# Rounding casts of converted weights moved to GpSimd, and five early copies to ScalarE, in a fused attention and expert kernel on one core

## The chip, the cores and the metric

The kernel runs on one core of a Trainium2 chip. The time is that of one execution on the device, in microseconds (us); the median of several runs is compared. A core has five engines, each with an instruction stream of its own, executed in order: TensorE (PE in the profile, its weight loads PEld), VectorE (DVE), ScalarE (ACT), GpSimd (POOL) and SyncE (SP, which here only issues DMAs). They meet by semaphores.

## The reference

Three stages, in fp32, on 4 batches of 576 positions, 2304 tokens in all:

```python
# attention: 8 heads of 64, window of 64 positions
scores = (q @ k.T) / sqrt(64); masked unless 0 <= i - j < 64
attn = exp(scores - max) / (sum + 1e-9);  x = attn @ v        # (2304, 512)
# dense layer: w_in (512, 2048), w_out (2048, 512)
h = x @ w_in;  g = h * tanh(softplus(h));  x = g @ w_out
# experts: 8, each w1 (512, 1024), w2 (1024, 512); one expert per token
e = argmax(x @ w_gate + modality_bias[modality])
out = gate[e] * (relu(x @ w1[e]) @ w2[e])
```

## The kernel before, in words

Large products are made of two-part numbers: a value is split into a high part (rounded to fp32r) and a low part (the rest), and three matmuls make one product (`hidden`, L338 to L342, and `output`, L377 to L379). So each weight has to be split first: the high part is a rounding copy, the low part is the value minus the high part.

The weights of the dense layer come from the host as 64-bit floats. A piece of 128x512 numbers is converted in `convert_a` by three operations on VectorE (a shift L300, and two that join masked words, L304 and L308), then `convert_b` makes the high part (L326, the line that the change touches) and hands back the arguments of the low part, which `convert_end` issues later on VectorE (L1004). There are 32 pieces. `convert_start(n)` issues n of the three operations; `convert_end` issues the low parts that are open, then the high parts of the pieces that are ready. Nothing is reordered: the schedule is the order in which the Python code issues.

Attention works in 36 steps of 64 positions. Step number `na` handles several positions in turn: scores for `na` (L142 adds the mask, L144), for the one before it the row maximum (VectorE, L159), its negation (GpSimd, L160) and four exponentials with their sums (ScalarE, L184), for the one before that the scaling: GpSimd adds 1e-9 to the sums (L198), VectorE takes the reciprocal (L199), GpSimd scales four blocks (L201). For the third position back TensorE turns the weights (`flip`, L211), a copy takes them out of PSUM (`flipped`, L216), and TensorE multiplies with the values (`values`, L227). `pt_copy` (L1016) chooses the engine of that copy: ScalarE if `na` is in `PT_ACT`, else VectorE. Then `done` copies the result (ScalarE, L239 with its low part L252 on VectorE for the first eight positions, later L245).

The first 12 steps (`PRE`) run attention alone, in `att_alone`, with a few operations of conversion: until about 45 us. The next 28 steps are mixed: each has one step of the dense layer (24 hidden matmuls, and from the third step on 12 output matmuls of the step two before), the activation (ScalarE L415 to L418 and L426, VectorE L420, L427, L428), the split of g (high part ScalarE L434, low part VectorE L435), one step of attention in two halves, `att_a` and `att_b`, and one piece converted in each half (`CONV` is 3), until the pieces are used up at about 155 us. In a half, the order is:

```python
def att_a(convs, *between):          # att_b: flipped, largest (L159, L160),
    ... done                         #   convert_end, convert_start, exps, values
    convert_end(); convert_start(convs)
    ... scale (L198, L199, L201), rest, scores, flip
```

After that come the rest of the dense layer, the routing and the experts.

Of the kernel before, what the change touches and what calls it, by code (L numbers as in the profile page):

```python
# [39 lines left out]
PRE = 12  # L40
AHEAD = 1
MASK_PE = 26
PT_ACT = range(PRE, 27)
RAW_AT = -1, 1, 3
V_AT = 1
REST = range(NG)
# [222 lines left out]
class Rounds:  # L269
# [43 lines left out]
    def convert_b(self, key, f):  # L313
        nc = self.nc
        src, j, half = key
        if src == "in":
            if j not in self.w1:
                self.w1[j] = self.w1_pool.tile([P, 2, KD, G], F32R, name="w1")
            hs = slice(2 * half, 2 * half + 2)
            parts = [self.w1[j][:, x, hs].rearrange("p a b -> p (a b)") for x in range(2)]  # L320
        else:
            if j not in self.w2:
                self.w2[j] = self.w2_pool.tile([P, 2, 2, D], F32R, name="w2")
            parts = [self.w2[j][:, x, half] for x in range(2)]
        hi, lo = parts
        nc.scalar.copy(hi, f)  # L326
        return lo, f, hi.bitcast(F32), ALU.subtract


# [603 lines left out]
def tile_kernel(tc, a):  # L933
    nc = tc.nc
    with ExitStack() as ctx:
# [22 lines left out]
        with tc.manual_schedule():  # L958
# [57 lines left out]
            def pt_copy():  # L1016
                if na in PT_ACT:
                    return nc.scalar.copy
                return nc.vector.tensor_copy
# [346 lines left out]
```

## Time and profile before

| | before |
|---|---|
| median of 3 runs | 748.85 us (747.72 to 749.16) |
| profiled execution | 749.38 us, of which the instructions span 747.6 us |
| TensorE (PE) busy | 719.3 us, 96% |
| VectorE (DVE) busy | 563.6 us, 75% |
| ScalarE (ACT) busy | 490.1 us, 66% |
| GpSimd (POOL) busy | 158.7 us, 21% |

The share of busy time is an average over stages. Times in the trace are counted from the start of the span. Matmuls are pipelined: the listed duration of one overlaps the next. On VectorE, too, an operation is listed as begun a little before the one ahead of it ends.

### The profile page before, as it was taken

To read this page: it belongs to the slowest core of one execution; us is meant where nothing else is said; L and a number is where in the kernel's file an instruction comes from. 1 tells how busy PE (TensorE), PEld (TensorE's weight loads), DVE (VectorE), ACT (ScalarE), POOL (GpSimd) and SP (SyncE) were. 2 spreads that over 40 slices of the span, in tenths; PEclk is the share of its full clock that TensorE was granted. 3 is DMA by queue.
4 is the path that set the end of the run, shared out by engine and by line. 5 is a ranking of instruction groups with operands and counts; after the bars stand their busy time and mean duration, and the time that the engine had idled before them with its cause. 6 is when DMAs were issued, how large, how long until landed. Compare 5 with 4: busy or idle time off the path is not lost. (4 is left out here: it accounts for less than half of the span.)

```text
span 747.6 us, 14044 instructions
## 1 busy us (share of the span) xinstructions
PE 719.3 (96%) x5123; PEld 648.6 (87%) x5123; DVE 563.6 (75%) x1323; ACT 490.1 (66%) x1018; POOL 158.7 (21%) x301
## 2 busy tenths in 40 slices
PE   5679999999999999999999999999999999999996
PEld 4568988998988899999998899998899999999995
DVE  4879999966565479889898988999987565555660
ACT  4568888888787677767776777676323546545452
POOL 5763223232322010101101011021123112220111
PEclk9999999999999999999999999999999999999999
DMA  8977667733241310000101000352011711111520
GB/s 258 270 218 229 218 211 225 219 122 79 78 121 58 120 53 1 29 29 29 58 1 37 21 29 29 113 168 59 30 57 57 268 43 58 57 39 34 198 86 32
DMA packets 42912, 75.51 MB, mean 101 GB/s; under 512 B 3857, under 2 KB 20241, under 8 KB 42706
## 3 DMA queue, kind: packets, MB, share of 16 engines
q1 hardware_dynamic: 30818, 56.01, 23.8%
q0 software_dynamic: 4480, 14.46, 5.7%
q10 hardware_dynamic: 7536, 4.06, 1.9%
q8 instruction: 42, 0.69, 0.4%
q14 instruction: 36, 0.29, 0.1%
HBM read 82.36 MB, written 13.39 MB: 128 GB/s over the span
## 5 line engine op out<-in xcount | busy, mean ns | idle before, releaser
L338 PE MATMUL h<-xh,w 128*128 128x256 f32 x576 | 166.8, 290 | 0.7 <-DVE y L428 0.7
L341 PE MATMUL h<-xl,w 128*128 128x256 f32 x576 | 163.6, 284 | 0.0
L342 PE MATMUL h<-xh,w 128*128 128x256 f32 x576 | 163.6, 284 | 0.0
L377 PE MATMUL acc<-w,g 128*128 128x512 f32 x288 | 115.4, 401 | 0.0
L338 PEld LDWEIGHTS h<-xh,w 128*128 128x128 f32 x576 | 110.9, 192 | 5.0 <-DVE y L428 1.1
L378 PE MATMUL acc<-w,g 128*128 128x512 f32 x288 | 112.6, 391 | 0.0
L341 PEld LDWEIGHTS h<-xl,w 128*128 128x128 f32 x576 | 111.1, 193 | 1.5
L379 PE MATMUL acc<-w,g 128*128 128x512 f32 x288 | 112.2, 390 | 0.0
L342 PEld LDWEIGHTS h<-xh,w 128*128 128x128 f32 x576 | 111.0, 193 | 0.0
L550 DVE CUSTOM_DVE_ANT_0 junk<-row,wg 128x512 bf16<-128x512 f32 x144 | 99.2, 689 | 2.7
L442 ACT ACTIVATE g<-h 128x512 fp32r<-128x512 f32 x36 | 21.5, 598 | 93.6 <-PE h L342 83.7
L341 PE MATMUL h<-xl,ew 128*128 128x256 f32 x288 | 81.6, 283 | 0.7 <-DVE xl L908 0.7
L342 PE MATMUL h<-xh,ew 128*128 128x256 f32 x288 | 81.5, 283 | 0.0
L338 PE MATMUL h<-xh,ew 128*128 128x256 f32 x288 | 81.5, 283 | 0.0
L415 ACT ACTIVATE y<-h 128x512 f32<-128x512 f32 x72 | 43.1, 599 | 58.0 <-PE h L342 56.2
L201 POOL TENSOR_SCALAR p<-p,r 128x128 f32<-128x128 f32 x144 | 64.1, 462 | 57.9 <-DVE r L199 54.1
L420 DVE SCALAR_TENSOR_TENSOR pq<-y,r 128x512 f32<-128x512 f32 x72 | 49.6, 689 | 28.9 <-ACT r L418 28.9
L629 POOL DMA_INDIRECT xs_dram<-row,posi x18 | 19.4, 1079 | 228.2 <-DVE row L620 92.2
L426 ACT ACTIVATE pq<-pq,mid 128x512 f32<-128x512 f32 x72 | 52.2, 726 | 22.9 <-DVE pq L420 18.7
L379 PEld LDWEIGHTS acc<-w,g 128*128 128x128 f32 x288 | 54.1, 188 | 11.9 <-DVE g L435 0.2
L435 DVE TENSOR_TENSOR g<-y,g 128x512 fp32r<-128x512 f32 x72 | 49.5, 687 | 17.6 <-ACT g L434 17.6
L377 PEld LDWEIGHTS acc<-w,g 128*128 128x128 f32 x288 | 54.3, 188 | 9.0
(216 smaller groups left out, 1653.2 us busy)
## 6 DMA issues: line engine op xcount, KB each, us to landing
s<-e_w SPq DMA_DIRECT2D x32, 1024.0 KB
v<-v SPq DMA_DIRECT2D x36, 256.0 KB
raw<-w_in SPq DMA_DIRECT2D x16, 512.0 KB
raw<-w_out SPq DMA_DIRECT2D x16, 512.0 KB
kt<-kT SPq DMA_DIRECT2D x17, 384.0 KB
qd<-qT SPq DMA_DIRECT2D x36, 128.0 KB
x_dram<-xs ACTq DMA_DIRECT2D x14, 256.0 KB
xraw<-x_dram SPq DMA_DIRECT2D x14, 256.0 KB
```

What stands on the lines that cost most here:

```text
L201: nc.gpsimd.tensor_scalar(p[:, c, :], p[:, c, :], r[:, c : c + 1], 0.0, ALU.mult, ALU.add)
L338: nc.tensor.matmul(h[:, f], w[:, 0, k, fs], xh[:, k], start=(k == 0), stop=False)
L341: nc.tensor.matmul(h[:, f], w[:, 0, k, fs], xl[:, k], start=False, stop=False)
L342: nc.tensor.matmul(h[:, f], w[:, 1, k, fs], xh[:, k], start=False, stop=(k == KD - 1))
L377: nc.tensor.matmul(acc[c], gh[:, 0, f, cs], w[:, 0, f], start=st, stop=False)
L378: nc.tensor.matmul(acc[c], gh[:, 0, f, cs], w[:, 1, f], start=False, stop=False)
L379: nc.tensor.matmul(acc[c], gh[:, 1, f, cs], w[:, 0, f], start=False, stop=en)
L415: nc.scalar.activation(y, h, AF.Tanh, scale=0.5)
L420: nc.vector.scalar_tensor_tensor(p, y, 1.0, r, ALU.add, ALU.mult)
L426: nc.scalar.activation(p, p, AF.Square, bias=self.c["mid"][:, 0:1])
L435: lo_engine.tensor_tensor(flat(t[:, 1]), g, flat(t[:, 0]).bitcast(F32), ALU.subtract)
L550: nc.vector.tensor_tensor_reduce(out=junk, in0=rows[c][:, 0:D], in1=self.wg[:, e], scale=1.0, scalar=0.0, op0=ALU.mult, op1=ALU.add, accum ...
```

## The change

The high part of the 32 converted pieces is made on GpSimd instead of ScalarE, and in five of the nine opening steps that have such a copy (4, 6, 8, 10, 11 of 3 to 11) the turned attention weights are copied by ScalarE instead of VectorE. Nothing else is changed.

```diff
-PT_ACT = range(PRE, 27)
+PT_ACT = 4, 6, 8, 10, 11, *range(PRE, 27)
...
         hi, lo = parts
-        nc.scalar.copy(hi, f)
+        nc.gpsimd.tensor_copy(hi, f)
         return lo, f, hi.bitcast(F32), ALU.subtract
```

GpSimd, in the mixed steps (L160 the negated maximum, L326 the casts, L198 the sums, L201 the scaling; the first rows belong to one step, the next to the step behind it):

```order
 L160 TENSOR_SCALAR mx_818<-mx_818 128x4
+L326 CAST w1_783<-cv_729 128x512
+L326 CAST w2_883<-cv_788 128x512
 L198 TENSOR_SCALAR r_891<-sm_838 128x4
 L201 TENSOR_SCALAR p_837<-p_837,r_891 128x128 x4
 L160 TENSOR_SCALAR mx_932<-mx_932 128x4
+L326 CAST w2_883<-cv_826 128x512
+L326 CAST w1_997<-cv_888 128x512
 L198 TENSOR_SCALAR r_1005<-sm_952 128x4
```

Two casts now stand one behind the other between the negated maximum and the sums of every mixed step with conversions.

ScalarE, at the start of the mixed steps (L216 the copy of the turned weights, L415 on the activation, L245 and L248 the attention output and its DMA):

```order
 L245 COPY xs_693<-o_659 128x4x64
-L326 CAST w2_695<-cv_589 128x512
 L216 COPY pt_719<-t_714 128x512
-L326 CAST w2_695<-cv_640 128x512
 L415 ACTIVATE y_732<-h_668 128x512
```

The copies of the turned weights no longer stand between two casts.

ScalarE, in the opening (L184 the exponentials, L239 the high part of the attention output):

```order
 L239 CAST xh_275<-o_358 128x4x64
-L326 CAST w1_386<-cv_243 128x512
 L184 ACTIVATE p_392,sm_393<-s_acc_326,mx_372 128x128 x4
+L216 COPY pt_405<-t_acc_381 128x512
 L239 CAST xh_275<-o_408 128x4x64
-L326 CAST w1_386<-cv_340 128x512
 L184 ACTIVATE p_441,sm_442<-s_375,mx_422 128x128 x4
```

The cast ahead of the four exponentials is gone, and the copy stands behind them. On VectorE the five copies (L216) leave the place behind the reciprocal (L199); all else there, and on TensorE, stays in its order.

## Rows read from the trace of the kernel before

**Rows 1.** Busy time by stage: from:to, us, each engine busy (instructions), granted clock, DMA share, GB/s

```profile
57.57:62.06 4.49, 4.49 (x25) 4.44 (x26) 3.98 (x7) 4.43 (x14) 0.82 (x3) 0.62 0.78 270
86.13:94.15 8.02, 8.02 (x67) 7.13 (x66) 7.72 (x15) 7.38 (x19) 2.48 (x6) 1.00 0.71 235
...
150.34:158.37 8.03, 8.03 (x68) 7.14 (x67) 5.86 (x12) 7.38 (x19) 2.68 (x6) 1.00 0.11 33
```

**Rows 2.** The casts by source line (ns min/median/max, first and last start); VectorE's copies

```profile
L326 ACT CAST w<-cv x32: 619/623/652, 23.9 to 152.6; 128x512 fp32r<-128x512 f32 x32
...
L216 DVE COPY pt<-t_acc 128x512 f32<-128x512 f32 x9 | 6.2, 685 | 2.0 <-PE t_acc L211 1.8
```

**Rows 3.** A steady mixed step in order of time: start, us, engine, what [idle before]

```profile
82.61 0.52 POOL L160 TENSOR_SCALAR mx<-mx 128x4 f32<-128x4 f32 x1 [0.20 <-DVE mx L159]
...
84.77 0.21 ACT L184 ACTIVATION_READ_ACCUMULATOR p<-s,mx 128x1 f32 x1
...
85.53 0.69 DVE L435 TENSOR_TENSOR g<-y,g 128x512 fp32r<-128x512 f32 x1 [0.21 <-ACT g L434]
...
86.13 0.39 PE L142 MATMUL s<-mask_b,eye 128*128 128x512 bf16 x1
...
88.40 0.17 DVE L199 RECIPROCAL r<-r 128x4 f32<-128x4 f32 x1
...
91.17 0.39 PE L338 MATMUL h<-xh,w 128*128 128x256 f32 x1
```

**Rows 4.** GpSimd alone and beside VectorE: in order of time, then by line

```profile
25.21 1.42 POOL L201 TENSOR_SCALAR p<-p,r 128x128 f32<-128x128 f32 x4 [0.38 <-PE t_acc L211]
...
46.97 3.05 POOL L201 TENSOR_SCALAR p<-p,r 128x128 f32<-128x128 f32 x4 [0.38 <-DVE r L199]
...
47.30 0.68 DVE L1004 TENSOR_TENSOR w<-cv,w 128x512 fp32r<-128x512 f32 x1
...
49.05 0.73 DVE L304 SCALAR_TENSOR_TENSOR cv<-raw,cv 128x512 int32<-128x512 int32 x1
...
50.00 0.22 POOL L160 TENSOR_SCALAR mx<-mx 128x4 f32<-128x4 f32 x1
...
L300 DVE TENSOR_SCALAR cv<-raw x32: 418/420/525, 13.2 to 147.8; 128x512 int32<-128x512 int32 x32
...
L519 POOL MEMSET room_row<- 128x256 f32 x1 | 0.3, 302 | 0.0
```

**Rows 5.** The opening, two steps of it, in order of time

```profile
25.34 0.69 DVE L216 COPY pt<-t_acc 128x512 f32<-128x512 f32 x1 [0.30 <-PE t_acc L211]
...
25.73 0.22 ACT L184 ACTIVATION_READ_ACCUMULATOR p<-s_acc,mx 128x1 f32 x1
...
27.93 0.69 DVE L304 SCALAR_TENSOR_TENSOR cv<-raw,cv 128x512 int32<-128x512 int32 x1
...
28.02 0.69 POOL L198 TENSOR_SCALAR r<-sm 128x4 f32<-128x4 f32 x1
...
28.88 0.69 DVE L216 COPY pt<-t_acc 128x512 f32<-128x512 f32 x1
```

**Rows 6.** The turnover to the mixed steps, ScalarE and TensorE, in order of time

```profile
49.19 0.62 ACT L326 CAST w<-cv 128x512 fp32r<-128x512 f32 x1
...
54.08 0.60 ACTq L248 DMA_DIRECT2D x_dram<-xs  x1
54.72 0.62 ACT L326 CAST w<-cv 128x512 fp32r<-128x512 f32 x1 [0.67 <-DVE cv L300]
...
55.87 0.56 ACT L216 COPY pt<-t 128x512 f32<-128x512 f32 x1
...
54.20 0.63 PE L211 MATMUL t<-ident,p 128*128 128x128 f32 x4
56.48 0.69 PE L227 MATMUL o<-pt,v 128*64 128x64 f32 x16 [1.66 <-ACT pt L216]
57.57 0.39 PE L338 MATMUL h<-xh,w 128*128 128x256 f32 x1 [0.40 <-DVE y L428]
```

## The prediction

> **What bounds the kernel now.** I read the busy time by stage first, then one step in order of time, then the places where GpSimd (POOL) and VectorE (DVE) run together, then the opening and the turnover.
>
> From 62.06 us on, TensorE sets the time. A step with conversions lasts 8.02 us and TensorE is busy in all of it; a step right after the conversions lasts 8.03 and is as full [rows 1]. So the rounding casts on ScalarE (ACT) cost nothing there: with or without them a step takes the same. But VectorE is busy 7.72 of the 8.02 us, which leaves 0.30 us, and 0.21 of that is one wait, for the high part of g [rows 1, 3]. The reader is to see that the second engine in line is VectorE, not the engine that the change relieves.
>
> Ahead of 62.06 it is otherwise. In the opening (attention alone, until 45 us) the chain is: turned weights done, copy, value matmuls. In the turnover TensorE stands idle for ScalarE and then for VectorE (1.66 and 0.40 us), and right behind it the granted clock is 0.62 over 4.49 us [rows 1, 6].
>
> The price of GpSimd beside VectorE is in [rows 4]. Four scalings take 1.42 us when nothing is in the way and 3.05 us at 46.97, beside the two-input operations of the conversion. The 4-column operation takes 0.22 us alone; at 82.61, where such an operation runs, it takes 0.52 and ends at 83.13 [rows 3, 4]. VectorE gives up little itself: the conversion's shift took at most 0.525 us against a median of 0.420, and the operation at 49.05 took 0.73 where the same one at 27.93 took 0.69 [rows 4, 5].
>
> **The opening: +2.1 us.** Five copies leave VectorE, 0.685 us each [rows 2]. None was late there: the copy at 25.34 starts when TensorE is done with turning [rows 5], so taking it from a busy VectorE gives nothing by itself. On ScalarE it stands behind the four exponentials of its step, which end at 25.95 [rows 5]. Without the 0.62 us cast ahead of them they may end some 0.3 earlier, held then by the row maximum: 25.65, and a copy of 0.56 [rows 6] ends at 26.21 instead of 26.03. That is 0.2 us on the chain, five times: 1.0. Four casts fall into the opening, at steps 6, 7, 9 and 10. At 7 and 9 the copy stays on VectorE, behind the reciprocal, which waits for the sum that GpSimd now prepares after a cast. At step 7 that sum is worked on from 28.02 to 28.71, to the end of the two-input operation at 27.93, and the copy starts at 28.88 [rows 5]. A cast ahead of it puts about 0.7 us on this copy. At step 9 I take 0.4, since the operation there ends earlier against the copy. Sum 1.0 + 1.1 = 2.1; ends 0 (copies no later, casts slip through) and 4 (0.5 on every ScalarE copy, 0.75 on both others).
>
> **The turnover: -2.7 us.** Two casts leave ScalarE on the path that TensorE waits for. The one at 49.19 stands ahead of a whole chain to the next copy; the one at 54.72 also waited 0.67 us for VectorE. Behind it come the square and the copy (55.87), and the value matmuls start at 56.48, though turning ended at 54.83 [rows 6]. Without the casts all of ScalarE's chain is about 0.5 earlier, so the issue of the output DMA ends near 54.2 instead of 54.68, the square runs right behind it, and the copy waits for turning alone, 54.85: value matmuls near 55.45, a gain of 1.0. The next hidden matmuls wait for the activation on VectorE, which follows the same square, and come at about 56.35 instead of 57.57: 1.2 in all. Behind this idle stretch the 24 matmuls and what is around them took 4.49 us at a granted share of 0.62 [rows 1], thus partly at the lower level of 1.2 GHz; without the drop they take about 3.0 (in a steady step the hidden matmuls run from 91.17 to the next scores, 8.02 us behind those at 86.13, which is 2.98 [rows 1, 3]). With an idle stretch half as long I expect no drop: 1.5 more. Ends: 0 (GpSimd, which is full from 46.97 to 50.02, holds the stage as long as ScalarE did) and -2.7.
>
> **The steady mixed steps: +3.5 us.** Two casts a step fall here; the last of the 32 began at 152.6 [rows 2], and (150.34 - 62.06)/8.02 makes 11 full steps.
> - A cast's price. No row has one on GpSimd. From below: a memset of 256 columns takes 302 ns [rows 4], two of them 0.60 us. From above: four scalings of 128 columns, 1.42 us. Between them: 0.355 us for 128 columns less 0.22 for 4 is 1.09 ns a column, 0.77 us for 512, of which 0.55 needs the memory path that VectorE also wants. I take this, since the scaling also reads and writes.
> - What gets through. From 47.30 to 49.78 VectorE ran four conversion operations in a row [rows 4]; three of the four scalings from 46.97 to 50.02, 0.14 us of streaming each, came through in that stretch and right behind it, and VectorE lost 0.10 + 0.04. So some 0.16 us of streaming passes in a microsecond, at 0.06 of VectorE's time.
> - What is queued. One cast stands behind the maximum (82.61 to 83.13), the other right behind it, then the sum, then the reciprocal's release. VectorE needs the first cast near 86.2 for a low part, behind the operation at 85.53, and the sum at 88.40 [rows 3]. These 5.2 us let 0.83 of the needed 1.10 us through and cost VectorE 0.31. For the other 0.27, and 0.14 for the sum behind it and waking, VectorE waits. 0.31 + 0.41 - 0.30 of slack = 0.42 us a step, 4.6 in 11 steps.
> - TensorE has a lead to lose first: it needs the exponentials (end 84.98) at 86.13 [rows 3], 1.15 us. That is paid once: 4.6 - 1.15 = 3.5.
>
> Ends: 0 (at the memset's 0.60 a cast has 0.4 us of streaming, two have 0.8, and 0.83 pass) and +8.8 (nothing passes: 1.10 + 0.10 - 0.30 = 0.9 a step). Were a cast as dear as four scalings, with 1.2 us of streaming, 2.40 - 0.83 + 0.31 + 0.14 - 0.30 makes 1.7 a step and +18.
>
> **A rule that speaks otherwise.** The rows say that a two-input operation on fp32 holds GpSimd up: the 4-column operation at 82.61 outlasts the subtraction before it. The Trainium skill, Advanced Engine Details and Errata, section VectorE Performance Modes, names only two-port Vector instructions as those that GpSimd instructions block and are blocked by. By that rule alone just the shift of each conversion would be in the way, the casts would run beside all else, and the third term would be 0; the whole would be -0.6, the time of the first rival below. The trace disagrees, with 0.52 us against 0.22; the page GPSIMD Engine Reference, section Key points, adds instructions with two SBUF inputs, and that fits the row.
>
> **Sum.** 2.1 - 2.7 + 3.5 = +2.9 us on the profiled execution's 749.4 us, which lies 0.5 above the median of the runs, 748.85. Forecast: **751.8 us**. The change does what it says: the order has all 32 casts on GpSimd and five copies on ScalarE, so I give no chance to its doing nothing.
>
> **Rivals.**
> - *The casts fit.* VectorE's 0.30 us and the gaps between operations hold both casts, so steady steps stay at 8.02. For it: the 4-column operation lost only 0.30 us. Against it: four scalings doubled their time, and the casts are longer. -0.6, thus 748.2.
> - *The casts fit and the opening loses nothing*, which is the other side: TensorE's wait for the copy at 55.87 is gone and nothing replaces it. It decides if no cast delays a low part or a reciprocal, that is, if a cast with its wait stays under about 2.5 us, half of the 5.2 above. Only the turnover's -2.7 is left: 746.2.
> - *GpSimd starves.* Nothing passes in the chain of two-input operations; every step grows by 0.9, the opening loses 3 and the clock drop stays (turnover -1.2): +10.6, thus 759.
>
> **How the numbers follow.** The forecast's case (749.5 to 756) has 0.40, starving 0.20, fitting 0.18, fitting with the opening free 0.22. A measurement of this kernel can tell about 0.2% from no change, 1.5 us: faster 0.22, same 0.18, slower 0.60. The range runs from 746 to 760.5: it holds the two lower rivals and the middle of the starving one, and leaves out the dear cast.
>
> **What would show it.** Right: GpSimd's casts at 0.8 us where VectorE is idle and 1.5 us or more in the steady steps; steps of about 8.4 us from 60 to 150, with TensorE idle in each and VectorE waiting for GpSimd at the low part or the reciprocal; the idle 1.66 us ahead of the value matmuls down to about 0.6, and no clock below 0.9 behind it. Wrong: steady steps still of 8.02 us, or casts that end within 1 us beside two-input operations; the term of 3.5 falls then. If value matmuls of the opening come as early as now, the 2.1 falls.

## The result, and the profile after

The changed kernel takes **755.59 us** (median of 6 runs, 753.03 to 756.71) against 749.0 for the kernel before on the same chip (6 runs, 747.72 to 749.66): ratio 1.0088, 95% interval 1.0070 to 1.0106. It is slower. The profiled execution took 755.6 us, of which the instructions span 753.8, 6.2 more than before.

The page of the changed kernel gives the busy time of each engine:

```profile
PE 721.1 (96%) x5123; PEld 649.2 (86%) x5123; DVE 568.0 (75%) x1318; ACT 476.9 (63%) x991; POOL 187.6 (25%) x333
```

ScalarE lost 13 us of work and GpSimd took 29 more. VectorE gained 4.4, although five copies left it.

To find the 6.2 us I cut the span at four of TensorE's instructions: the mask matmul (L142) of opening step 5, the first hidden matmul (L338) of the first mixed step, the mask matmul of the third mixed step, and the one 11 steps later. In the changed kernel they are:

```profile
21.00 0.39 PE L142 MATMUL s_acc<-mask_b,eye 128*128 128x512 bf16 x1
...
48.17 0.58 PE L338 MATMUL h<-xh,w 128*128 128x256 f32 x1
...
63.78 0.39 PE L142 MATMUL s<-mask_b,eye 128*128 128x512 bf16 x1
...
156.50 0.39 PE L142 MATMUL s<-mask_b,eye 128*128 128x512 bf16 x1
```

The same cut for every kernel of this study, in us; the last two columns are the time from the start of the first to the end of the last of the 24 hidden matmuls in the first and in the third mixed step, 3.1 at full clock:

| kernel | start | opening | turnover | 11 steady steps | 1st | 3rd |
|---|---|---|---|---|---|---|
| before | 20.01 | 25.10 | 16.95 | 88.29 | 3.14 | 4.64 |
| after | 21.00 | 27.17 | 15.60 | 92.73 | 4.31 | 3.13 |
| e1_casts_only | 19.11 | 26.17 | 14.37 | 92.77 | 3.14 | 3.12 |
| e2_copies_only | 19.67 | 25.83 | 17.15 | 88.28 | 4.35 | 3.13 |
| e3_mixed_pool | 19.25 | 25.09 | 14.38 | 92.73 | 3.15 | 3.13 |
| e4_rest_first | 19.50 | 23.62 | 16.92 | 88.29 | 3.13 | 4.61 |
| e5_mixed_half | 19.91 | 25.09 | 15.24 | 88.30 | 3.14 | 3.14 |
| e6_no11 | 19.38 | 28.65 | 15.86 | 92.69 | 4.62 | 3.13 |
| e7_turnover_only | 20.35 | 23.62 | 14.38 | 88.39 | 3.13 | 3.14 |
| e8_after_again | 19.55 | 26.91 | 15.93 | 92.71 | 4.64 | 3.14 |

After minus before: +1.0 start, +2.07 opening, -1.35 turnover, +4.44 steady steps: 6.2, the whole difference of the spans.

**Steady steps.** The busy time by stage (columns as in [rows 1]), for a mixed step with conversions and for one behind them:

```profile
89.08:97.51 8.43, 8.10 (x68) 7.14 (x67) 8.33 (x15) 5.99 (x17) 4.49 (x8) 1.00 0.67 220
156.53:164.55 8.02, 8.02 (x68) 7.13 (x67) 7.11 (x13) 6.62 (x19) 3.58 (x8) 1.00 0.11 33
```

A step grew from 8.03 to 8.43 us and TensorE is busy 8.10 of it; VectorE is busy 8.33, where it was 7.72 [rows 1]. Behind the conversions a step takes 8.02, as before. The full step in order of time (columns as in [rows 3]) shows where VectorE got the additional time:

```profile
94.52 0.39 PE L338 MATMUL h<-xh,w 128*128 128x256 f32 x1 [0.33 <-DVE y L428]
...
95.22 0.52 POOL L160 TENSOR_SCALAR mx<-mx 128x4 f32<-128x4 f32 x1 [0.20 <-DVE mx L159]
...
95.58 0.68 DVE L308 SCALAR_TENSOR_TENSOR cv<-raw,cv 128x512 int32<-128x512 int32 x1
...
95.70 1.79 POOL L326 CAST w<-cv 128x512 fp32r<-128x512 f32 x2
...
96.18 0.83 DVE L300 TENSOR_SCALAR cv<-raw 128x512 int32<-128x512 int32 x1
...
97.05 0.98 DVE L304 SCALAR_TENSOR_TENSOR cv<-raw,cv 128x512 int32<-128x512 int32 x1
...
97.58 0.54 POOL L198 TENSOR_SCALAR r<-sm 128x4 f32<-128x4 f32 x1
...
101.42 0.17 DVE L199 RECIPROCAL r<-r 128x4 f32<-128x4 f32 x1
```

The two casts stand in a row beside L308, L300 and L304. L300 takes 0.83 instead of 0.42 [rows 4], L304 0.98 instead of 0.69 [rows 5]: 0.70 us more, without any wait at a semaphore. In the second half of the step, where no cast stands, neither is longer than before. The reciprocal has no wait ahead of it. TensorE waits 0.33 us in each step, for VectorE's y.

The same by source line (columns as in [rows 2]); the two indented rows are the waits for GpSimd of VectorE's low part (L1004) and reciprocal (L199), us and times:

```profile
L326 POOL CAST w<-cv x32: 602/812/1157, 25.1 to 162.1; 128x512 fp32r<-128x512 f32 x32
...
L300 DVE TENSOR_SCALAR cv<-raw x32: 412/472/846, 13.0 to 155.2; 128x512 int32<-128x512 int32 x32
...
L304 DVE SCALAR_TENSOR_TENSOR cv<-raw,cv x32: 681/713/987, 15.2 to 156.1; 128x512 int32<-128x512 int32 x32
...
  POOL w L326: 0.7, 1
...
  POOL r L198: 7.6, 9
```

**Opening.** Steps 6 and 7 in order of time, and the end of the stage. L252 is the low part of the attention output, L216 the copies:

```profile
26.60 0.59 ACT L216 COPY pt<-t_acc 128x512 f32<-128x512 f32 x1
...
26.99 2.64 POOL L201 TENSOR_SCALAR p<-p,r 128x128 f32<-128x128 f32 x4 [0.38 <-DVE r L199]
...
29.60 0.22 POOL L160 TENSOR_SCALAR mx<-mx 128x4 f32<-128x4 f32 x1
...
29.77 0.60 POOL L326 CAST w<-cv 128x512 fp32r<-128x512 f32 x1
...
30.46 0.23 POOL L198 TENSOR_SCALAR r<-sm 128x4 f32<-128x4 f32 x1
...
30.72 0.18 DVE L199 RECIPROCAL r<-r 128x4 f32<-128x4 f32 x1 [1.33 <-POOL r L198]
30.81 0.68 DVE L216 COPY pt<-t_acc 128x512 f32<-128x512 f32 x1
...
41.96 2.61 POOL L201 TENSOR_SCALAR p<-p,r 128x128 f32<-128x128 f32 x4 [0.38 <-DVE r L199]
...
44.54 0.65 POOL L160 TENSOR_SCALAR mx<-mx 128x4 f32<-128x4 f32 x1
...
45.22 0.37 ACT L184 ACTIVATE p<-s,mx 128x128 f32<-128x128 f32 x1 [1.55 <-POOL mx L160]
...
46.61 0.59 ACT L216 COPY pt<-t_acc 128x512 f32<-128x512 f32 x1
...
47.25 0.99 PE L227 MATMUL o<-pt,v 128*64 128x64 f32 x16 [2.30 <-ACT pt L216]
```

From mask matmul to mask matmul, steps 5 to 10 take 3.61, 3.25, 4.67, 3.26, 3.85 and 3.55 us, and step 11 takes 4.98 to the first hidden matmul (before: 3.54 each, the last 3.86). Most of the time is lost at steps 7 and 11. At 7, a scaling of 2.64 us, the maximum, the cast and the sum stand in a row on GpSimd; VectorE's reciprocal waits 1.33 us for the sum, and the copy stands behind it. At 11 the maximum stands behind a scaling of 2.61, ScalarE waits 1.55 us for it, and the copy, now behind the exponentials, lets TensorE wait 2.30 us. The value matmuls behind that wait take 0.99 us, where the same 16 took 0.69 before: the fall of the clock that the next stage shows begins here, and 0.3 us of the opening's 2.07 is its work.

**Turnover and clock.** Three stretches by stage: the first and third mixed step's hidden matmuls, and the start. Under them, in order of time, TensorE's waits at the start and in the turnover:

```profile
48.19:52.34 4.15, 4.15 (x27) 4.15 (x26) 3.00 (x6) 0.38 (x1) 3.69 (x7) 0.68 0.85 276
60.80:63.79 2.99, 2.99 (x25) 2.94 (x26) 2.96 (x5) 2.93 (x12) 2.78 (x5) 1.00 0.93 333
15.38:21.00 5.62, 3.91 (x33) 3.17 (x30) 2.74 (x7) 2.46 (x10) 3.64 (x9) 0.70 1.06 291
```

```profile
16.81 2.05 PE L144 MATMUL s<-kt,qd 128*128 128x128 f32 x8 [1.04 <-DMA qd<-qT]
...
59.76 0.28 PE L227 MATMUL o<-pt,v 128*64 128x64 f32 x2 [0.76 <-ACT pt L216]
...
60.80 0.39 PE L338 MATMUL h<-xh,w 128*128 128x256 f32 x1 [0.36 <-DVE y L428]
```

Ahead of the value matmuls TensorE waits 0.76 us instead of 1.66 [rows 6], and the hidden matmuls behind them run at a granted clock of 1.00 instead of 0.62 [rows 1]. But the first mixed step, behind the 2.30 us above, now runs at 0.68. The start has a wait of 1.04 us for a load and a clock of 0.70, in a stretch where the change moves only the copy of step 4.

### The profile page after: what moved, and what is told of

It reads as the page before. It is cut to its first block, busy times and chain, and to the rows that moved or that the text cites. A ratio compares the mean times of both kernels' runs of the same rounds, so it can differ in the third digit from the quotient of the medians.

```text
span 753.8 us, 14044 instructions
## 1 busy us (share of the span) xinstructions
PE 721.1 (96%) x5123; PEld 649.2 (86%) x5123; DVE 568.0 (75%) x1318; ACT 476.9 (63%) x991; POOL 187.6 (25%) x333
## 5 line engine op out<-in xcount | busy, mean ns | idle before, releaser
L338 PE MATMUL h<-xh,w 128*128 128x256 f32 x576 | 166.6, 289 | 4.5 <-DVE y L428 4.3
L338 PEld LDWEIGHTS h<-xh,w 128*128 128x128 f32 x576 | 110.7, 192 | 9.7 <-DVE y L428 6.4
L201 POOL TENSOR_SCALAR p<-p,r 128x128 f32<-128x128 f32 x144 | 66.8, 480 | 60.9 <-DVE r L199 60.1
L338 PE MATMUL h<-xh,ew 128*128 128x256 f32 x288 | 81.5, 283 | 0.0
L415 ACT ACTIVATE y<-h 128x512 f32<-128x512 f32 x72 | 43.1, 599 | 58.2 <-PE h L342 53.5
L379 PEld LDWEIGHTS acc<-w,g 128*128 128x128 f32 x288 | 54.1, 188 | 12.0 <-DVE g L435 0.2
L377 PEld LDWEIGHTS acc<-w,g 128*128 128x128 f32 x288 | 54.3, 189 | 9.0
L378 PEld LDWEIGHTS acc<-w,g 128*128 128x128 f32 x288 | 54.4, 189 | 8.6
```

The lines of the kernel that those rows point to most:

```text
L201: nc.gpsimd.tensor_scalar(p[:, c, :], p[:, c, :], r[:, c : c + 1], 0.0, ALU.mult, ALU.add)
L338: nc.tensor.matmul(h[:, f], w[:, 0, k, fs], xh[:, k], start=(k == 0), stop=False)
L377: nc.tensor.matmul(acc[c], gh[:, 0, f, cs], w[:, 0, f], start=st, stop=False)
L378: nc.tensor.matmul(acc[c], gh[:, 0, f, cs], w[:, 1, f], start=False, stop=False)
L379: nc.tensor.matmul(acc[c], gh[:, 1, f, cs], w[:, 0, f], start=False, stop=en)
L415: nc.scalar.activation(y, h, AF.Tanh, scale=0.5)
```

## The experiments

**One half of the change, then the other.**

e1_casts_only, on the kernel before:

```diff
-        nc.scalar.copy(hi, f)
+        nc.gpsimd.tensor_copy(hi, f)
```

> The kernel before with the 32 casts on GpSimd; the nine opening copies stay on VectorE. Theory path: while a cast streams on GpSimd, an operation of VectorE that reads or writes by two SBUF paths is held; the two casts of a step hold the shift and the first joining operation behind it by 0.70 us together, so a steady mixed step lasts 7.72 + 0.70 = 8.42 us, as in the changed kernel. Theory queue: VectorE waits at semaphores for casts and sums that come late; then VectorE shows idle time at L1004 and L199 in these steps. In the opening the four steps with a cast lose 0.3 to 1.1 us each and no step gains. Time 755 to 758 us by path; under 752 if the five copies, not the casts, made the loss.

Measured: 751.58 us (750.80 to 755.41, 9 runs), ratio 1.0049 (1.0032 to 1.0066). The steady steps lose 4.48, the opening 1.07 (0.24 to 0.28 at each of the steps 6, 7, 9 and 10), and the turnover gains 2.58: in neither mixed step does the clock fall. So all of the steady loss is the casts', and the gain forecast for the turnover is real where the opening ends without a long wait. The time itself missed what was expected: 755 to 758 if the casts made the loss, under 752 if the copies did. Taken alone it would blame the copies; the stages show why it doesn't. The steady steps lose what the casts were expected to cost, but the expectation had left out the turnover's gain.

e2_copies_only, on the kernel before:

```diff
-PT_ACT = range(PRE, 27)
+PT_ACT = 4, 6, 8, 10, 11, *range(PRE, 27)
```

> The kernel before with the five opening copies on ScalarE, the casts on ScalarE as before. Steady mixed steps must last 8.02 us. Theory release: the value matmuls of an opening step wait not only for the copy but for the low part of the attention output (L252), which stands behind the copy on VectorE and frees the PSUM tile; then a step whose copy is on ScalarE is shorter, about 3.25 us instead of 3.54 where no cast stands ahead of the exponentials, and 747.5 to 749 us result. Theory copy (the prediction's): the copy behind the exponentials comes 0.2 us later, and at the two steps with a cast on ScalarE later still: 750 to 751 us.

Measured: 749.49 us (748.20 to 753.35, 10 runs), ratio 1.0013 (0.9994 to 1.0031): no difference that can be told, and between the two times expected (747.5 to 749, and 750 to 751), so the steps have to decide. Opening steps 5 to 11 take 3.61, 3.55, 3.61, 3.25, 3.61, 3.55 and 4.64. Where no cast stands ahead of the exponentials (step 8) the ScalarE copy makes the step 0.29 *shorter*; at step 11 it costs 0.78, TensorE waits 2.00 us there, and the fall of the clock comes in the first mixed step (4.35) instead of the third (3.13). So with the copies alone the fall changes place. It is not the shorter wait that spares the third step here, for that wait is as long as before:

```profile
58.14 0.69 PE L227 MATMUL o<-pt,v 128*64 128x64 f32 x16 [1.66 <-ACT pt L216]
```

The two halves do not simply add. By stage they make +1.80 in the opening and -2.38 in the turnover; the whole change makes +2.07 and -1.35. The casts alone bring no fall, the copies alone only move one; together the moved fall is an additional one. And at step 7 the casts alone cost 0.24, the copies alone 0.07, both 1.13. The four scalings of step 6 show what the copies do there, first in e1_casts_only, then here:

```profile
25.01 1.42 POOL L201 TENSOR_SCALAR p<-p,r 128x128 f32<-128x128 f32 x4 [0.38 <-DVE r L199]
```

```profile
24.95 2.65 POOL L201 TENSOR_SCALAR p<-p,r 128x128 f32<-128x128 f32 x4 [0.38 <-PE t_acc L211]
```

Without the copy, VectorE comes to its next two-input operation (L1004) 0.66 us behind the start of the scalings instead of 1.26, and they take 2.65 instead of 1.42. In the changed kernel the cast and the sum of step 7 stand behind these longer scalings.

**Where the casts move.** e3_mixed_pool: casts on GpSimd only from step 12 (`PRE`) on, no copies moved.

```diff
-    def convert_b(self, key, f):
+    def convert_b(self, key, f, pool):
...
-        nc.scalar.copy(hi, f)
+        (nc.gpsimd.tensor_copy if pool else nc.scalar.copy)(hi, f)
...
-                    low_parts.append((key, R.convert_b(key, f)))
+                    low_parts.append((key, R.convert_b(key, f, na >= PRE)))
```

> The kernel before with only the 28 casts from the first mixed step on on GpSimd; the opening is as before. Path: steady steps of 8.43 us, 11 times 0.41 = 4.5 us lost, and the turnover gains 1.2 us and, if the granted clock does not fall, 1.5 more: 750.8 to 752.3 us. Queue: the same loss only if VectorE shows idle time before L1004 or L199.

Measured: 751.35 us (750.16 to 753.56, 9 runs), ratio 1.0037 (1.0024 to 1.0049), as expected. The opening is that of before, the turnover gains 2.57, the steady steps lose 4.44. So in these two stages casts that move only there do what they did in e1. Without the start the stages of the profiled execution make +1.9 us; the medians differ by 2.9, and that execution, 750.16, is the fastest of the nine.

**What the value matmuls of the opening wait for.** Before, they start at 26.47 with 1.16 us of idle time that has no releaser, 0.44 behind the end of the copy of 25.34 [rows 5]. In that gap stands L252, which reads the attention output of the step before out of the one PSUM tile that the value matmuls write. In order of time, kernel before:

```profile
25.95 0.41 DVE L252 TENSOR_TENSOR xl<-o,xh 128x256 fp32r<-128x256 f32 x1
...
26.47 0.69 PE L227 MATMUL o<-pt,v 128*64 128x64 f32 x16 [1.16 <-issue]
```

e4_rest_first issues L252 ahead of the copy (`rest` ahead of `flipped` in `att_alone`), with the casts and copies of before:

```diff
+                    A.rest()
...
-                A.rest()
```

> The kernel before with one order changed: in the opening the low part of the attention output (L252) is issued ahead of the copy of the turned weights (L216) on VectorE, both engines and all casts as before. Release: the value matmuls then wait for the copy alone and come 0.34 us earlier in each of 8 steps, 2.7 us in all, about 746.3 us. Copy: nothing changes, 749 us, or slower by up to 1 us if the low part delays the copy.

Measured: 746.80 us (744.73 to 747.28, 10 runs), ratio 0.9973 (0.9962 to 0.9983). The opening gains 1.48, less than expected (2.7): steps 5, 6 and 9 gain 0.38 each, but at 7, 10 and 11 the copy itself comes late, and they gain 0.07 at most. In order of time:

```profile
24.12 0.39 DVE L252 TENSOR_TENSOR xl<-o,xh 128x256 fp32r<-128x256 f32 x1
...
24.45 0.69 DVE L216 COPY pt<-t_acc 128x512 f32<-128x512 f32 x1
```

The value matmuls now follow the copy, with 0.78 us of idle time. This shows L252 as the hidden second wait. It also fits that a ScalarE copy shortens a step: with it, L252 goes off earlier on VectorE. TensorE's wait in the turnover stays at 1.66, and so does the fall of the clock behind it (4.61).

**Does the length of the cast set the loss?** e5_mixed_half: in the mixed steps GpSimd casts columns 0 to 255 and ScalarE the rest.

```diff
-        nc.scalar.copy(hi, f)
+        if pool:
+            m = f.shape[-1] // 2
+            nc.gpsimd.tensor_copy(hi[:, :m], f[:, :m])
+            nc.scalar.copy(hi[:, m:], f[:, m:])
+        else:
+            nc.scalar.copy(hi, f)
...
-                    low_parts.append((key, R.convert_b(key, f)))
+                    low_parts.append((key, R.convert_b(key, f, na >= PRE)))
```

> In the mixed steps GpSimd casts the first 256 columns of each piece and ScalarE the other 256; the opening is as before. Path: what holds VectorE is the time that the casts stream, so half the columns hold it for about 0.35 us a step instead of 0.70: 7.72 + 0.35 = 8.07, steps of 8.03 to 8.10 us, and the run is back within 1 us of the kernel before, less the turnover's gain of ScalarE time, if that is still there: 746.5 to 749 us. If instead each cast costs a fixed time per instruction, the steps stay near 8.4 and the time near 751 us.

Measured: 748.16 us (746.82 to 749.95, 10 runs), ratio 0.9992 (0.9981 to 1.0003), as expected. A steady step takes 8.03 us again. Of the 1.71 us that the turnover gains in the profiled execution, 747.21, the medians show 0.6. By stage, and then in order of time (the cast is L328 here):

```profile
92.39:100.42 8.03, 8.03 (x68) 7.14 (x67) 7.93 (x15) 6.64 (x20) 3.77 (x8) 1.00 0.67 210
```

```profile
98.31 1.36 POOL L328 CAST w<-cv 128x256 fp32r<-128x256 f32 x2
...
98.79 0.62 DVE L300 TENSOR_SCALAR cv<-raw 128x512 int32<-128x512 int32 x1
...
99.44 0.77 DVE L304 SCALAR_TENSOR_TENSOR cv<-raw,cv 128x512 int32<-128x512 int32 x1
```

L300 and L304 are held 0.20 and 0.08, together 0.28 instead of 0.70, which goes into VectorE's 0.30 of slack [rows 1]: 7.93 busy of 8.03. The number of casts is the same, so the loss grows with their length, and it costs time only where it exceeds the slack.

**Is it the copy of step 11 that moves the clock fall?** e6_no11, the changed kernel with that copy back on VectorE:

```diff
-PT_ACT = 4, 6, 8, 10, 11, *range(PRE, 27)
+PT_ACT = 4, 6, 8, 10, *range(PRE, 27)
```

> The changed kernel with the copy of opening step 11 back on VectorE (ScalarE copies 4, 6, 8 and 10). Theory: at step 11 the ScalarE copy waits for exponentials that are late, since GpSimd gets to the negated maximum only after a scaling that a cast had delayed; TensorE then idles 2.30 us and the granted clock falls in the next 24 matmuls. With the copy on VectorE the value matmuls of step 11 come 0.8 us earlier and the clock stays at its upper level: 2 us faster than the changed kernel, about 753.6 us, first mixed matmuls in 3.1 instead of 4.3 us. Rival: the late part is the reciprocal on VectorE, and the copy is as late there: 755.6 us.

Measured: 755.10 us (752.20 to 759.25, 5 runs), ratio 1.0089 (1.0054 to 1.0124). Nothing is gained over the changed kernel, and the theory falls. Step 11 is shorter, 4.15 us instead of 4.98, but TensorE still waits 1.78 us in it (the copy on VectorE is late as well, behind the reciprocal), and the first mixed step still runs slowly (4.62). The scalings ahead of the late maximum still take 2.61 us (at 42.64): the copy of step 10, which is still on ScalarE, no longer stands between them and VectorE's two-input operations. In e1, with that copy on VectorE, they took 1.42 (at 39.94). In the profiled execution a second fall came, behind a wait of 1.91 us in step 7. By stage:

```profile
27.00:31.00 4.00, 1.93 (x26) 1.46 (x26) 2.63 (x7) 1.50 (x8) 3.44 (x10) 1.00 0.87 272
31.00:35.00 4.00, 3.27 (x25) 2.85 (x26) 3.75 (x8) 2.46 (x10) 3.53 (x6) 0.56 0.57 182
35.00:39.00 4.00, 3.50 (x23) 2.94 (x19) 0.58 (x2) 1.78 (x9) 2.50 (x8) 0.59 0.70 245
39.00:43.00 4.00, 2.38 (x29) 2.08 (x29) 3.85 (x9) 2.15 (x10) 2.15 (x5) 1.00 0.74 222
```

The changed kernel has the same wait of 1.91 us at step 7, and its clock stayed at 1.00 behind it. A fall behind such a wait is thus not certain: it comes in some executions. The spread of these runs goes with the clock: the mean granted clock of the whole execution was 0.996 in the run of 752.20 us and 0.987 in that of 759.25.

**A version that beats both.** e7_turnover_only has e4's order, no copies moved, and GpSimd casts in the first two mixed steps alone:

```diff
-        nc.scalar.copy(hi, f)
+        (nc.gpsimd.tensor_copy if pool else nc.scalar.copy)(hi, f)
...
-                    low_parts.append((key, R.convert_b(key, f)))
+                    low_parts.append((key, R.convert_b(key, f, na in (PRE, PRE + 1))))
...
+                    A.rest()
...
-                A.rest()
```

> The kernel with the low part ahead of the copy in the opening, and GpSimd casts in the first two mixed steps alone; all other casts on ScalarE. Theory: there TensorE waits for ScalarE, so moving these four casts gains 1.2 us and, as the idle stretch halves, the granted clock stays up, 1.4 us more; the steady steps stay at 8.03 us: 744.2 us. Rival: the clock still falls, 745.6 us; or the casts on GpSimd delay the first steps as much as they relieve, 746.8 us.

Measured: **744.94 us** (744.60 to 746.22, 4 runs), ratio 0.9952 (0.9936 to 0.9969): faster than both kernels. By stage, a steady step and the third mixed step's hidden matmuls:

```profile
90.46:98.49 8.03, 8.03 (x68) 7.14 (x66) 7.77 (x15) 6.68 (x18) 2.53 (x6) 1.00 0.73 229
55.36:58.50 3.14, 3.14 (x25) 3.10 (x26) 3.10 (x5) 3.08 (x12) 2.13 (x5) 1.00 0.85 303
```

Opening -1.48, turnover -2.57, steady +0.10; no clock below 1.00 in either stretch. Both gains that the theory names came; 744.2 us was expected.

**Was the +1.0 us at the start the change's?** e8_after_again is the changed kernel, unedited.

> The changed kernel once more, to see which idle stretches and falls of the granted clock come back: the steady steps of 8.43 us must; a fall in the first 24 mixed matmuls (4.31 us instead of 3.14) is expected, since the idle stretch of 2.30 us ahead of it comes from the order; the wait of 1.04 us for a load at 16.8 us and the fall behind it should not return if it was chance.

Measured: 755.10 us (754.15 to 756.05, 2 runs), ratio 1.0090 (1.0066 to 1.0113). The start takes 19.55 and the wait for the load is gone. Steps of 8.43 and the slow first mixed step (4.64, behind the same 2.30 us) are back. Over the ten executions the start lies between 19.11 and 21.00 without order by kernel, and e7 has such a wait for a load (1.06 us) at full clock; the 1.0 belongs to that execution.

## Why the prediction was right or wrong

The forecast of 751.8 us had the direction right, and 755.59 lies in its range. The sum was +2.9; the profiled execution gives +6.2, of which 1.0 is the start. The rest, 5.2 against 2.9, goes by terms.

**Opening, +2.1: measured +2.07, the size right by luck, the working mostly wrong.** "0.2 us on the chain, five times" did not come: where no late maximum and no ScalarE cast is ahead, a ScalarE copy takes 0.28 off the step (3.25 and 3.26 at steps 6 and 8), since the value matmuls wait for L252 too, which stood behind the copy (e4). The late sum at steps 7 and 9 was right in kind, but a cast ahead of it, priced at 0.7 and 0.4, costs 0.24 and 0.28 by itself (e1); at step 7 it is 1.13, where the copies have made the scalings ahead of it longer as well (e2). What I missed is step 11, 1.12: the copy behind exponentials that wait for a maximum behind a scaling, 0.3 of it the fallen clock. The copies alone cost 0.78 there (e2).

**Turnover, -2.7: measured -1.35.** The step that failed is the one from "With an idle stretch half as long I expect no drop" to "1.5 more". For the place it speaks of the forecast came: 0.76 us of wait, and no fall (e1, e3 and e7 give the -2.57 to -2.58 whole). But the changed kernel has a fall all the same, in the step that I had not looked at, the first mixed one, 1.17 us (4.31 against 3.14), behind the opening's new wait of 2.30 us. I had priced the opening's delay and the clock as two things; in all four executions with 1.78 us or more ahead of the first mixed step (this one, e2, e6, e8) the clock fell there, and in none of the others. That the length of the wait is the whole cause is not shown: with 1.66 us in the third step it fell before and in e4, not in e2.

**Steady steps, +3.5: measured +4.44.** The step of 8.4 us came (8.43), with TensorE idle in each and VectorE full. Two parts of the term were wrong. First the mechanism: "For the other 0.27, and 0.14 for the sum behind it and waking, VectorE waits" did not happen: the low part waits for a cast once in the whole kernel, 0.7 us; the reciprocal waits for GpSimd 9 times, 7.6 us, all of it ahead of 60 us. Between 60 and 160 us neither has a wait. All 0.70 us is inside L300 and L304, so 7.72 + 0.70 = 8.42 sets the step. Second, "TensorE has a lead to lose first ... 1.15 us": it was measured at the exponentials, but TensorE waits for y, and there the hidden matmuls of the third mixed step are late already (0.36 here, 0.40 before [rows 6]). There was no lead; 11 times 0.40 is the whole 4.4.

The cast's price was too high: 0.77 was taken, 0.60 measured (29.77), nothing else near it. "1.5 us or more in the steady steps" was wrong as well: both together take 1.79, and the median of the 32 is 0.81. By my own sign, "casts that end within 1 us beside two-input operations", the term should have fallen. The term came all the same, so the sign looked at the wrong engine: the loss is inside VectorE's operations, not in late casts. That the casts still cost 0.70 a step is because the two engines take turns. The listed times fit this. L308 ends at 96.26 and the first cast at 96.73 (1.03 us from 95.70), 0.47 later; L300 ends at 97.01, 0.42 of work of its own counted back from there begins at 96.59, 0.14 ahead of the cast's end. The second cast ends at 97.49, 0.48 behind L300; L304 ends at 98.03, its own 0.69 counted back begins at 97.34. In e5 the halves end 0.26 behind L308 and L300 (99.13 and 99.67). By these times each waits until the other's instruction is nearly done. VectorE loses 0.70 us a step to casts that end 0.95 behind it, in e5 0.28 to 0.52: in both, some 0.25 less than the casts' own time. My picture, a share of streaming that passes while both run, gave the right size by chance: 0.42 a step forecast, 0.40 measured.

The Trainium skill, SBUF — State Buffer, section SBUF: two separate sides, says it that way: the port pair that VectorE and GpSimd share is an exclusive lock, held for a whole instruction, also against VectorE operations with two SBUF inputs if the GpSimd operation reads SBUF. The trace agrees in the main: what a cast still needs behind the VectorE operation ahead of it is 0.47 us for 512 columns and 0.26 for 256. The narrower rule that I weighed in the prediction would leave L304 unheld; it is held 0.29.

**Rivals.** That the casts fit fell with the steps of 8.43; e5 shows where they would: at half the length. GpSimd did not starve, a step grew by 0.40 and not by 0.9. The rival on the other side named the turnover's -2.7 as a gain without cost; e7 has that gain, with casts in two steps alone.

What stays open: the stages of the execution of e8 add up to +5.2 without the start, while the medians differ by 6.6. The clock points at more falls in the other runs. Averaged over the whole execution it is 0.997 or 0.998 where the trace has no fall in the stages above (e1, e3, e5, e7), 0.995 or 0.996 with one (before, e2, e4, e8), 0.993 with two (the changed kernel, one of them in the start). Of the six runs of the changed kernel the fastest, 753.03, had 0.996; the other five, 755.16 to 756.71, had 0.992 to 0.994. Where their falls came no trace shows.

## What to carry to other kernels

Before an operation is moved to GpSimd, add its length to VectorE's busy time in that stage, and not only to GpSimd's, as an upper estimate: beside VectorE's conversion the cast that is 0.60 us alone cost up to 0.41 us of VectorE, and two half casts a step fitted into 0.30 us of slack. Look at what leaves the other engine too: a copy moved off VectorE let its next two-input operation run into GpSimd's scalings, 2.65 us instead of 1.42. Move it only in the stage where the engine that gives it up is waited for (e7: two steps of 28 gave the whole gain of the turnover). And where a matmul's wait has no releaser, look for who still reads the PSUM tile that it writes.

## What was not expected of the hardware

Falls of the granted clock moved with the waits of TensorE. Behind waits of 1.66 us ahead of the third mixed step (before, e4) and of 1.78 to 2.30 us ahead of the first (the changed kernel, e2, e6, e8), the next hidden matmuls took 4.3 to 4.6 us instead of 3.1; where both waits are 0.75 to 1.51 us long (e1, e3, e5, e7) they ran at full clock. The rows have 0.62 and 0.68 over such stretches, and 0.5 of the full clock is the lower level, 1.2 GHz, so they ran partly at it. But the length of the wait alone does not decide: behind 1.91 us in step 7 the clock fell in e6, but not in the changed kernel (nor in e8, 1.92), and behind 1.66 us in the third mixed step of e2 it stayed at 1.00.
